# Moving the input tiles and four weight loads to other DMA queues in a linear-attention and MLP mixer

## The chip, the core and the metric

The kernel runs on one core of a Trainium2 chip. The core has five engines with a program each: TensorE (PE, matmuls; its weight loads are listed as PEld), VectorE (DVE), ScalarE (ACT), GpSimd (POOL) and SyncE (SP). Transfers between the main memory and the on-chip memory, and transposes by DMA, are issued by an engine into that engine's queue: SyncE and ScalarE have a hardware queue each (q1 and q10 in the profile), GpSimd a software one (q0). All queues are served by the same 16 DMA engines. An engine's issues go out in program order, and each may wait for semaphores first.

The metric is the device time of one execution in microseconds (us). Three runs of the kernel before took 259.40, 259.89 and 271.33 us; the median is 259.89.

## The reference

There are 2048 tokens of 640 features. A gate mixes two branches of the same input x:

```python
g = sigmoid((x * gate_w).sum(-1, keepdims=True))
a = A_ref(x, A_wqkv, A_wo)
b = B_ref(x, B_w1, B_w2, B_w3, B_w4)
return g * a + (1 - g) * b

# A: linear attention, 32 heads of 20
q, k, v = heads(x @ wqkv)
pq, pk = phi(q), phi(k)          # phi(t) = where(t > 0, t + 1, exp(t)) + 1e-6
kv = einsum("bhsd,bhse->bhde", pk, v);  z = pk.sum over tokens
o = (pq @ kv) / (pq . z + 1e-6)
a = o @ wo
# B: shifted MLP
h = gelu(layernorm(x) @ w1)      # its four quarters are shifted by +1, -1, +2, -2 tokens
x1 = x + shifted(h) @ w2
b = x1 + gelu(layernorm(x1) @ w3) @ w4
```

The inputs are bf16. w1 and w2 are 640 x 640, w3 is 640 x 1728, w4 is 1728 x 640, wqkv is 640 x 1920.

## The kernel before

Tokens are worked on in 16 tiles of 128. Features lie on the 128 partitions in 5 blocks, so a product over 640 features is 5 matmuls.

**Order.** The program records each operation with what it reads and writes; semaphore waits follow from overlaps of these. The order on each engine is that of recording. The loads and turns of x and a few constants are recorded first, line by line (lines 692 to 762). Everything after that is an item with a planned duration and due times (`IT.add`), and `_Items.run` chooses the next item by a cost model. An item that holds only DMAs takes its place on its queue by this choice. A wait at the head of an engine's program holds up all that was recorded behind it on that engine.

**Phase A** (to about 53 us): x tiles are loaded token by token into `x_tok` (`load_x`, line 680). Tiles 0 to 2 are transposed on PE. Tiles 3 to 15 are transposed by DMA from `x_tok` into `xT` on SyncE (`x_turn`, line 689): one "turn" per tile. There are four turn semaphores, so turn t waits for turn t - 4. Per tile, `q_tile` and `k_tile` multiply the turned tile (as PE's loaded weights) with wq and wk; ScalarE takes the exponential and VectorE finishes phi. Once per four tiles `q_turned` makes the last 128 q features, which a DMA turn (`q_back`, from `mT` to `pq_tok`) brings back to token order.

**Phase B** (to about 77 us): PE accumulates G = x^T pk (`gt_step`, `gt_tail`; part of it comes back by a DMA turn into `GT`, line 825), and `kvt_group` (line 993) multiplies G with wv into the heads' kv. Meanwhile GpSimd normalises x tiles into three slots `xn` (`normalize`), and SyncE turns them into `xnT` (`t_xn`, line 871).

**Phase C**: `w1_group` and `w2_tile` make x1; the second layer norm is turned in the same manner; `w3_group`, `w4_tile` and the attention's product with `M_sb` make the output. `m_last` and `m_first` read wo.

**Loads.** The weights of q and k are loaded at the start over the queues of SyncE and ScalarE. w1, w2, wv and wo are loaded over GpSimd's queue in three items (`lw1`, `lw2`, `lwv`): 8, 8 and 6 issues, each item behind the phi of key tile 7, 9 or 11 (`k_done`). w3 and w4 are loaded over SyncE's queue in two items (`w3load`, `w4load`) that stand behind the last turns of the first layer norm; w4 lies in memory that phase A and B use for other things, w3 in memory of its own.

Of the kernel before, what the change touches and what calls it, by code (L numbers as in the profile page):

```python
# [11 lines left out]
D = 640  # L12
F = 1728
H = 32
DH = 20
NT = S // 128
NCH = S // 512
# [5 lines left out]
B3 = 60  # L23
# [393 lines left out]
def _build(nc, A_x, A_wqkv, A_wo, B_w1, B_w2, B_w3, B_w4, gate_w, out, dbg=None, stop=None):  # L417
    sch = _Sched(nc)
# [55 lines left out]
    w3 = pa.alloc("w3", [128, KD, F], BF16)  # L474
    w1 = pa.alloc("w1", [128, KD, D], BF16)
    w2 = pa.alloc("w2", [128, KD, D], BF16)
    wo_aug = pa.alloc("wo_aug", [128, 6, D], BF16)
    x_tok = pa.alloc("x_tok", [128, NT, D], BF16)
# [23 lines left out]
    wv = wvf[:, 0:KD * D].rearrange("p (k d) -> p k d", d=D)  # L502
# [159 lines left out]
    def memset(engf, ap, val):  # L662
        return engf(lambda e: e.memset(ap, val), [], [ap])
# [11 lines left out]
    x2 = A_x[0]  # L675

    def dma_in(out_ap, in_ap, key, **kw):
        return sch.dma("sp", out_ap, in_ap, key, **kw)

    def load_x(t):  # L680
        dma_in(x_tok[:, t, :], x2[128 * t:128 * (t + 1), :], "x%d" % t)

    def load_wq(k, queue):
        sch.dma(queue, wq[:, k, 0:512], A_wqkv[128 * k:128 * (k + 1), 0:512], "wq%d" % k)

# [3 lines left out]
    def x_turn(t):  # L689
        sch.dma("sp", xT[:, :, 128 * t:128 * (t + 1)], x_tok[:, t, :], "trx%d" % (t % 4), transpose=True)  # L690

    gwr = xn[:, 1, 0:128]
    dve(lambda e: e.memset(gwr, 0.0), [], [gwr])
    load_x(0)
    load_wq(0, "act")
    load_x(1)
    load_wq(1, "act")
    load_wq(2, "sp")
    load_wq(3, "act")
    load_x(2)  # L700
# [6 lines left out]
    load_wk(2, "sp")  # L707
    load_wk(4, "sp")
    load_x(4)
    x_turn(3)  # L710
    load_x(5)
    sch.dma("pool", xn[0:KD, 1, 0:128], gate_w.rearrange("(k p) -> k p", p=128), "gw")
    x_turn(4)
    x_turn(5)
    for t0, t1 in ((6, 10), (10, NT)):
        dma_in(x_tok[:, t0:t1, :], x2[128 * t0:128 * t1, :].rearrange("(n p) d -> p n d", p=128), "xc%d" % t0)
        for t in range(t0, t1):
            x_turn(t)

    k_done = {}  # L720

    def load_w1():
        dp = [k_done[7]]
        for g_ in range(4):
            sch.dma("pool", w1[:, :, 128 * g_:128 * (g_ + 1)],
                    B_w1[:, 160 * g_:160 * g_ + 128].rearrange("(k p) f -> p k f", p=128), "w1", group_total=8, deps=dp)
            sch.dma("pool", w1[:, :, 512 + 32 * g_:512 + 32 * (g_ + 1)],
                    B_w1[:, 160 * g_ + 128:160 * (g_ + 1)].rearrange("(k p) f -> p k f", p=128), "w1", group_total=8, deps=dp)

    def load_w2():  # L730
        dp = [k_done[9]]
        for g_ in range(4):
            sch.dma("pool", w2[:, g_, :], B_w2[160 * g_:160 * g_ + 128, :], "w2", group_total=8, deps=dp)
            sch.dma("pool", w2[32 * g_:32 * (g_ + 1), 4, :], B_w2[160 * g_ + 128:160 * (g_ + 1), :], "w2", group_total=8, deps=dp)

    def wo_rows(h, e, ns):
        v = A_wo[0:600, :].rearrange("(q p) d -> p q d", p=B3)
        q0 = 2 * h + e
        return v[:, q0:q0 + 4 * (ns - 1) + 1:4, :]

    def load_wvo():
        dp = [k_done[11]]
        sch.dma("pool", wv[:, :, :], A_wqkv[:, 2 * D:3 * D].rearrange("(k p) f -> p k f", p=128), "wv", deps=dp)
        for h in range(2):
            for e in range(2):
                ns = 3 - h
                sch.dma("pool", wo_aug[64 * h:64 * h + B3, e:e + 2 * ns - 1:2, :],
                        wo_rows(h, e, ns), "wo", group_total=5, deps=dp)
        sch.dma("pool", wo_aug[64:104, 4, :], A_wo[600:D, :], "wo", group_total=5, deps=dp)

    memset(pool, ones_c[:], 1.0)
    memset(pool, wkg[:, :, D:D + 1], 1.0)
# [7 lines left out]
    memset(pool, wvf[:, KD * D:], 0.0)  # L760
    memset(pool, hsT[:, :, 0:4], 0.0)
    memset(pool, hsT[:, :, S:S + 4], 0.0)


    tags = {}
# [7 lines left out]
    IT = _Items()  # L773
# [41 lines left out]
    def gt_tail(t):  # L815
        if t == 0:
            gt_bank["t"] = pair()
            bank_hold.update((gt_bank["t"], gt_bank["t"] + 1))
        b = gt_bank["t"]
        for o, n0, n1 in ((ps[:, b, 0:512], 0, 512), (ps[:, b + 1, 0:128], 512, D)):  # L820
            gt_acc(o, [(pk_tok[:, t, 512:D], x_tok[:, t, n0:n1])], t)
        if t == NT - 1:
            bank_hold.difference_update((b, b + 1))
            activation(Mt[:, :], psf[:, 512 * b:512 * b + D], ACTF.Copy)
            sch.dma("sp", GT[:, :, 512:D], Mt[:, :], "trg", transpose=True)
# [45 lines left out]
    def t_xn(which, t):  # L871
        sx = xn_slots[(which, t)]
        tag_chk("xn", sx, (which, t))
        sch.dma("sp", xnT[:, :, 128 * t:128 * (t + 1)], xn[:, sx, :], "trn%d" % slot("trn", 4), transpose=True)
# [66 lines left out]
    def addA(name, dur, fn, deps=()):  # L941
        IT.add("A", name, dur, fn, deps)
# [7 lines left out]
    for i in range(3, NT + 2):  # L950
        if i < NT:
            addA(("q", i), 1.08, lambda t=i: q_tile(t))
            addA(("k", i), 1.36, lambda t=i: k_tile(t))
            if i % 4 == 3:
                addA(("qx", i // 4), 1.08, lambda c=i // 4: q_turned(c))
                IT.add("QB", ("qb", i // 4), 0.0, lambda c=i // 4: q_back(c),
                       deps=[(("qx", i // 4), 2.5), (("t1", NT - 1), 0.0) if i == NT - 1 else (("k", i + 1), 0.0)])
        if i > 3:
            for t in range(3) if i == 4 else (i - 2,):
                addA(("g0", t), 0.27, lambda t=t: gt_tail(t), deps=[(("k", max(t, 1)), 2.0)])  # L960

    IT.add("LW", ("lw1",), 0.0, load_w1, deps=[(("k", 7), 0.0)])
    IT.add("LW", ("lw2",), 0.0, load_w2, deps=[(("k", 9), 0.0)])
    IT.add("LW", ("lwv",), 0.0, load_wvo, deps=[(("k", 11), 0.0)])

    def stats1(c):
        ln_chunk_stats(st1, c, lr[:, 4 * c:4 * c + 4, 0:1].rearrange("p t o -> p (t o)"))
# [140 lines left out]
    def w3_group(c, j):  # L1108
        cols = slice(512 * c, 512 * (c + 1))
        sl = c % 2  # L1110
        if j == 0:
            tag_set("h2T", sl, c)
        b = bank()
        mm_group(ps[:, b, :], [(w3[:, k, 128 * j:128 * (j + 1)], xnT[:, k, cols]) for k in range(KD)])
        activation(h2T[:, j, 512 * sl:512 * (sl + 1)], ps[:, b, :], ACTF.Gelu_apprx_tanh)
# [177 lines left out]
        for n0, n1 in ((0, 384), (384, D)) if t0 == NT - 1 else ((0, D),):  # L1293
            sch.dma("act" if n1 == 384 else "sp", dst[:, :, n0:n1], x_tok[:, t0:t1, n0:n1], "out%d" % slot("out", 4))

    def w3_load():
        dma_in(w3[:, :, 0:F], B_w3.rearrange("(k p) f -> p k f", p=128), "w3")

    def w4_load():
        dma_in(w4[:, 0:KFF, :], B_w4[0:128 * KFF, :].rearrange("(k p) f -> p k f", p=128), "w4a")  # L1300
        dma_in(w4[0:64, KFF, :], B_w4[128 * KFF:F, :], "w4b")
        dma_in(w4[64:128, KFF, :], B_w4[128 * KFF:F, :], "w4c")
# [3 lines left out]
    for c in range(NCH):  # L1306
        for j in range(KD):
            deps = [(("t1", u), 0.9) for u in range(4 * c, 4 * c + 4)] if j == 0 else []
# [7 lines left out]
    for t in range(NT):  # L1316
        c = t // 4
        deps = [(("w1", c, KD - 1), GEL)]
# [8 lines left out]
    for u in range(NT):  # L1327
        deps = [(("s2", u // 4), 3.2 + 0.9 * (u % 4))]
# [3 lines left out]
            deps.append((("t1", NT - 3 + u), 0.0))  # L1332
        IT.add("N2", ("n2", u), 0.0, lambda u=u: normalize(2, u, st2), deps)
        IT.add("T2", ("t2", u), 0.0, lambda u=u: t_xn(2, u), deps=[(("n2", u), 1.1)] + ([(("mt",), 0.0)] if u == 12 else []))
    IT.add("MISC", ("w3load",), 0.0, w3_load, deps=[(("qb", NCH - 1), 0.0), (("k", NT - 1), 0.0), (("t1", NT - 1), 0.0)])
    IT.add("MISC", ("w4load",), 0.0, w4_load, deps=[(("qb", NCH - 1), 0.0), (("kvt", 1), 0.0), (("t1", NT - 1), 0.0), (("z", NT - 1), 1.5)])
    for c in range(NCH):
        for j in range(KFF):
            deps = []
            if c == 0 and j == 0:  # L1340
                deps0 = [(("kvt", 1), 0.0), (("z", NT - 1), 1.5)]
            else:
                deps0 = []
            if j == 0:
                deps = deps0 + [(("t2", u), 0.9) for u in range(4 * c, 4 * c + 4)]
                deps.append((("w3load",), 0.0))
                if c >= 2:
                    deps.append((("w4", (5, 11)[c - 2]), 0.0))
            if c == 0 and j == 3:
                deps.append((("w2", NT - 1), 0.0))  # L1350
            if c == 1 and 7 <= j <= 10:
                deps.append((("a", j - 7), 0.0))
            IT.add("W3", ("w3", c, j), 1.08, lambda c=c, j=j: w3_group(c, j), deps)
            if c == 1 and j == KFF - 1:
                for c2 in (0, 2):
                    IT.add("W3", ("w3h", c2), 1.14, lambda c2=c2: w3_half(c2), [(("t2", u), 0.9) for u in range(4 * c2 + 4, 4 * c2 + 8)] + [(("a", 3), 0.0)])
                IT.add("W3", ("w4h", 0), 0.76, lambda: w4_half(0), [(("w4load",), 0.0), (("a", 3), 0.0)])
    for t in range(NT):
        deps = [(("zb",), 1.0), (("q", max(t, 2)), 2.0), (("sg", 1), 0.0)]
# [13 lines left out]
    for t in range(NT):  # L1373
        g = GOF[t]
        t0, t1 = GROUPS[g]
        cl = (t1 - 1) // 4
        deps = [(("qt", t), 3.0), (("w4load",), 0.0), (("m", 1), 1.0), (("mt",), 2.5)]
# [65 lines left out]
```

## Time and profile before

The profiled execution took 259.2 us; its span, from the first instruction to the last, is 257.9 us.

| | |
|---|---|
| granted clock of TensorE | 1.00 in the whole span |
| DMA moved | 26.50 MB, mean 103 GB/s |
| SyncE's queue (q1) | 21.87 MB, 40.2% of the 16 engines' span |
| GpSimd's queue (q0) | 3.28 MB, 5.8% |
| ScalarE's queue (q10) | 1.11 MB, 1.4% |
| w3, 2160 KB, issued at 87.89 us | 8.1 us from issue to landing |
| w4's main part, 2080 KB, issued right behind it | 15.2 us |
| x tiles 6 to 9, 640 KB | 4.6 us |
| x tiles 10 to 15, 960 KB | 5.3 us |
| turns of x (xT) | 2.6 to 7.2 us, median 2.7 |

An engine's busy time counts its instructions but not its sequencer's work: waits, branches, DMA issues. All of SyncE is sequencer, so it has no busy time; its rows tell when a DMA was issued and how long the issue took. The time from issue to landing is that of one DMA, with the time that it stood behind others in its queue. The chain is followed back from the last instruction to whatever released each step.

### The profile page before, as it was taken

To read this page: it belongs to the slowest core of one execution; us is meant where nothing else is said; L and a number is where in the kernel's file an instruction comes from. 1 tells how busy PE (TensorE), PEld (TensorE's weight loads), DVE (VectorE), ACT (ScalarE), POOL (GpSimd) and SP (SyncE) were. 2 spreads that over 40 slices of the span, in tenths; PEclk is the share of its full clock that TensorE was granted. 3 is DMA by queue.
4 is the path that set the end of the run, shared out by engine and by line. 5 is a ranking of instruction groups with operands and counts; after the bars stand their busy time and mean duration, and the time that the engine had idled before them with its cause. 6 is when DMAs were issued, how large, how long until landed. Compare 5 with 4: busy or idle time off the path is not lost.

```text
span 257.9 us, 3904 instructions
## 1 busy us (share of the span) xinstructions
PE 255.1 (99%) x1478; PEld 126.7 (49%) x1478; DVE 144.8 (56%) x289; ACT 108.9 (42%) x224; POOL 90.9 (35%) x144
## 2 busy tenths in 40 slices
PE   8999999999999999999999999999999999999996
PEld 4555555544454545555444445444444744444744
DVE  2697888899964995589999300399700033200033
ACT  1587676651366868666854331001540100253100
POOL 5020499976952162677908000123200021300000
PEclk9999999999999999999999999999999999999999
DMA  7856699956637699372628630114130022200012
GB/s 226 226 135 114 188 137 177 262 109 126 127 76 79 125 399 293 84 100 56 121 49 117 123 60 3 31 25 127 36 17 0 3 52 80 102 1 3 0 20 102
DMA packets 57650, 26.50 MB, mean 103 GB/s; under 512 B 48884, under 2 KB 56221, under 8 KB 57632
## 3 DMA queue, kind: packets, MB, share of 16 engines
q1 hardware_dynamic: 54800, 21.87, 40.2%
q0 software_dynamic: 1168, 3.28, 5.8%
q10 hardware_dynamic: 1664, 1.11, 1.4%
q8 instruction: 11, 0.18, 0.3%
q14 instruction: 7, 0.06, 0.1%
HBM read 12.04 MB, written 2.62 MB: 57 GB/s over the span
## 4 chain that ended last, share of the span: by engine, by line
PE 99%; DVE 0%; issue 0%
PE ps L604 53%; PE ps L1213 30%; PE ps L811 8%; PE ps L922 2%; PE ps L884 1%; PE ps L1240 1%; PE ps L1128 1%; PE ps L615 1%; PE ps L1009 0%; PE ps L1038 0%; PE ps L923 0%; DVE x_tok L643 0%
## 5 line engine op out<-in xcount | busy, mean ns | idle before, releaser
L604 PE MATMUL ps<-xnT,w 128*128 128x512 bf16 x360 | 81.3, 379 | 0.0
L643 DVE SCALAR_TENSOR_TENSOR x_tok<-ps,stg,abx 128x512 bf16<-128x512 f32 (+2 forms) x17 | 12.2, 718 | 81.4 <-PE ps L1213 81.3
L660 ACT ACTIVATE h2T<-ps 128x512 bf16<-128x512 f32 x52 | 30.6, 598 | 59.5 <-PE ps L604 59.5
L604 PEld LDWEIGHTS ps<-xnT,w 128*128 128x128 bf16 x360 | 34.5, 98 | 39.8 <-issue 0.5
L1213 PE MATMUL ps<-w,h2T 128*128 128x512 bf16 (+2 forms) x221 | 45.4, 366 | 0.0
L626 POOL TENSOR_SCALAR xn<-x_tok,st 128x640 bf16<-128x640 bf16 x32 | 36.0, 1130 | 25.4 <-DMA xnT<-xn 24.9
L626 POOL TENSOR_SCALAR abx<-x_tok,stg 128x640 f32<-128x640 bf16 x16 | 15.3, 965 | 70.7 <-DVE x_tok L643 70.7
L1213 PEld LDWEIGHTS ps<-w,h2T 128*128 128x128 bf16 x221 | 21.2, 98 | 23.5
L660 ACT ACTIVATE Er<-ps 128x512 bf16<-128x512 f32 (+1 forms) x36 | 23.0, 649 | 14.6 <-PE ps L604 10.3
L659 ACT ACTIVATE junk<-x_tok 128x640 bf16<-128x640 bf16 x32 | 23.6, 738 | 3.9 <-DVE x_tok L641 3.7
L660 ACT ACTIVATE hsT<-ps 128x512 bf16<-128x512 f32 (+1 forms) x32 | 19.0, 594 | 12.5 <-PE ps L604 12.0
L604 PE MATMUL ps<-w,hsT 128*128 128x512 bf16 (+1 forms) x160 | 23.7, 299 | 0.0
L604 PE MATMUL ps<-wkg,xT 128*128 128x130 bf16 (+1 forms) x140 | 21.4, 299 | 0.0
L641 DVE SCALAR_TENSOR_TENSOR x_tok<-ps,x_tok 128x640 bf16<-128x640 f32 x16 | 13.1, 821 | 11.2 <-PE ps L604 10.5
L604 PEld LDWEIGHTS ps<-w,hsT 128*128 128x128 bf16 x160 | 13.3, 98 | 12.3
L1213 PE MATMUL ps<-M_sb,pqnT 128*128 128x512 bf16 (+2 forms) x85 | 18.6, 367 | 0.0
L811 PE MATMUL ps<-pk_tok,x_tok 128*128 128x512 bf16 x80 | 17.8, 379 | 0.0
L604 PEld LDWEIGHTS ps<-wkg,xT 128*128 128x128 bf16 x140 | 11.9, 97 | 11.4
L1157 DVE TENSOR_TENSOR pq_tok<-pq_tok,dnr 128x300 bf16<-128x300 bf16 (+1 forms) x48 | 16.9, 405 | 0.5
L634 DVE TENSOR_TENSOR qprod<-qprod,pk_tok 128x640 f32<-128x640 f32 x13 | 16.3, 1252 | 0.4
L626 DVE TENSOR_SCALAR Er<-Er 128x512 bf16<-128x512 bf16 (+1 forms) x36 | 12.3, 341 | 6.9 <-ACT Er L660 6.2
L604 PE MATMUL ps<-wq,xT 128*128 128x512 bf16 x65 | 16.2, 379 | 0.0
(87 smaller groups left out, 243.8 us busy)
## 6 DMA issues: line engine op xcount, KB each, us to landing
w<-in_B_w_dram SPq DMA_DIRECT2D x1, 2160.0 KB, 8.1
w<-in_B_w_dram SPq DMA_DIRECT2D x1, 2080.0 KB, 15.2
out_dram<-x_tok SPq DMA_DIRECT2D x3, 640.0 KB, 3.2
w<-in_B_w_dram POOLq DMA_DIRECT2D x8, 160.0 KB, 6.4
x_tok<-in_A_x_dram SPq DMA_DIRECT2D x6, 160.0 KB, 3.7
x_tok<-in_A_x_dram SPq DMA_DIRECT2D x1, 960.0 KB, 5.3
wv<-in_A_wqkv_dram POOLq DMA_DIRECT2D x1, 800.0 KB, 5.7
x_tok<-in_A_x_dram SPq DMA_DIRECT2D x1, 640.0 KB, 4.6
```

What stands on the lines that cost most here:

```text
L604: ins = e.matmul(out_ap, l, r, start=(i == 0), stop=(i == n - 1))
L615: ins = e.transpose(o, s_, ident[:])
L626: return engf(lambda e: e.tensor_scalar(out_ap, in_ap, s1, s2, op0, op1), rd, [out_ap], cost=cost)
L634: return engf(lambda e: e.tensor_tensor(out_ap, a, b_, op), [a, b_], [out_ap], cost=cost)
L641: return dve(lambda e: e.scalar_tensor_tensor(out_ap, in0, scalar, in1, op0, op1, accum_out=accum), rd, [out_ap, accum], cost=cost + 70.0)
L643: return dve(lambda e: e.scalar_tensor_tensor(out_ap, in0, scalar, in1, op0, op1), rd, [out_ap], cost=cost)
L659: return act(lambda e: e.activation(out_ap, in_ap, func, bias=bias, scale=scale, accum_out=accum), rd, wr, cost=cost)
L660: return act(lambda e: e.activation(out_ap, in_ap, func, bias=bias, scale=scale), rd, wr, cost=cost)
L811: ins = e.matmul(o, l, r, start=(t0 + q_ == 0), stop=(t0 + q_ == NT - 1))
L922: ins = e.matmul(ps[:, b, 0:512], l, w[:, k, 0:512], start=(k == 0), stop=(k == KD - 1))
L1157: dve(lambda e, o=o, i0=i0, i1=i1: e.tensor_tensor(o, i0, i1, ALU.mult), [i0, dnr[:, 1, sd, :]], [o], cost=cost)
L1213: ins = e.matmul(o, l, r, start=first and i == 0, stop=last and i == len(prs) - 1, skip_group_check=True)
```

## The change

Three things move; no operation on data is added or removed.

- x tile 5 (160 KB) and x tiles 6 to 9 (640 KB) are loaded over ScalarE's queue, behind the loads that stand there already. They wait for nothing.
- x tiles 10 to 15 (960 KB) are still loaded over SyncE's queue, now between turns 7 and 8 instead of behind turn 9.
- w1, w2, wv, wo and w3 are loaded over SyncE's queue, recorded behind the constants, so they stand behind turn 15 on that queue and wait for no other engine. The three items of GpSimd's loads and the item of w3 are gone; the first `w3_group` no longer names w3's item as a condition, the wait for the data remains. w4 is loaded as before.

Per engine, the instructions of PE, VectorE and ScalarE keep their order, apart from the two new issues on ScalarE ahead of its first table load. GpSimd loses its 22 issues, and eight of its normalisations come ahead of the last statistics of the first layer norm, where it was one. On SyncE the 23 issues stand between turn 15 and the first turn of `mT`; behind the three turns of `mT` come eight turns into `xnT`, then the turn into `GT`, then four more (before: the turn into `GT`, then ten).

```diff
+    def load_xs(queue, t0, t1):
+        sch.dma(queue, x_tok[:, t0:t1, :], x2[128 * t0:128 * t1, :].rearrange("(n p) d -> p n d", p=128), "xc%d" % t0)
...
     load_x(4)
-    x_turn(3)
-    load_x(5)
+    load_xs("act", 5, 6)
+    load_xs("act", 6, 10)
     sch.dma("pool", xn[0:KD, 1, 0:128], gate_w.rearrange("(k p) -> k p", p=128), "gw")
-    x_turn(4)
-    x_turn(5)
-    for t0, t1 in ((6, 10), (10, NT)):
-        dma_in(x_tok[:, t0:t1, :], x2[128 * t0:128 * t1, :].rearrange("(n p) d -> p n d", p=128), "xc%d" % t0)
-        for t in range(t0, t1):
-            x_turn(t)
+    for t in range(3, 8):
+        x_turn(t)
+    load_xs("sp", 10, NT)
+    for t in range(8, NT):
+        x_turn(t)
...
     def load_w1():
-        dp = [k_done[7]]
         for g_ in range(4):
-            sch.dma("pool", w1[:, :, 128 * g_:128 * (g_ + 1)],
-                    B_w1[:, 160 * g_:160 * g_ + 128].rearrange("(k p) f -> p k f", p=128), "w1", group_total=8, deps=dp)
-            sch.dma("pool", w1[:, :, 512 + 32 * g_:512 + 32 * (g_ + 1)],
-                    B_w1[:, 160 * g_ + 128:160 * (g_ + 1)].rearrange("(k p) f -> p k f", p=128), "w1", group_total=8, deps=dp)
+            dma_in(w1[:, :, 128 * g_:128 * (g_ + 1)],
+                   B_w1[:, 160 * g_:160 * g_ + 128].rearrange("(k p) f -> p k f", p=128), "w1", group_total=8)
+            dma_in(w1[:, :, 512 + 32 * g_:512 + 32 * (g_ + 1)],
+                   B_w1[:, 160 * g_ + 128:160 * (g_ + 1)].rearrange("(k p) f -> p k f", p=128), "w1", group_total=8)
...
     memset(pool, hsT[:, :, S:S + 4], 0.0)
+    load_w1()
+    load_w2()
+    load_wvo()
+    dma_in(w3[:, :, 0:F], B_w3.rearrange("(k p) f -> p k f", p=128), "w3")
...
-    IT.add("LW", ("lw1",), 0.0, load_w1, deps=[(("k", 7), 0.0)])
-    IT.add("LW", ("lw2",), 0.0, load_w2, deps=[(("k", 9), 0.0)])
-    IT.add("LW", ("lwv",), 0.0, load_wvo, deps=[(("k", 11), 0.0)])
...
-    def w3_load():
-        dma_in(w3[:, :, 0:F], B_w3.rearrange("(k p) f -> p k f", p=128), "w3")
...
-    IT.add("MISC", ("w3load",), 0.0, w3_load, deps=[(("qb", NCH - 1), 0.0), (("k", NT - 1), 0.0), (("t1", NT - 1), 0.0)])
...
-                deps.append((("w3load",), 0.0))
```

`load_w2` and `load_wvo` change as `load_w1` does.

## The prediction

> **What bounds the kernel now.** I read the page first: the span, the busy shares and the chain that ended last.
>
> ```profile
> span 257.9 us, 3904 instructions
> PE 255.1 (99%) x1478; PEld 126.7 (49%) x1478; DVE 144.8 (56%) x289; ACT 108.9 (42%) x224; POOL 90.9 (35%) x144
> PE 99%; DVE 0%; issue 0%
> ```
>
> TensorE is on the chain from end to end. A busy PE need not be a fast one, so the pace comes next, from the chain in order of time (start, length, what; this stretch holds the places that the change can reach late).
>
> ```profile
> 69.82 4.32 PE ps L604 x20
> 74.13 1.08 PE ps L811 x5
> 75.21 1.08 PE ps L604 x5
> 76.29 1.06 PE ps L1009 x50
> ```
>
> Twenty 512-column matmuls in 4.32 us are 0.216 us each; no stretch of the chain after 12 us is slower per matmul, and the waits of PE list one wait, 0.8 us at the start. The changed program issues the same PE, DVE and ACT compute in the same order, so the time falls only if the first 12 us shrink. There, L922 takes 1.67 us for 7 and 1.88 us for 8 matmuls, 0.3 us above 15 x 0.216; that 0.3 us is the largest gain to be had, and the change brings nothing earlier that those matmuls read. What remains is a loss: wherever a transfer is late for PE, PE has no later idle time to make it up, and the loss stands in the end time.
>
> So I read for each moved transfer when PE needs it. SyncE's own rows (issues; "us" runs to the end of the last of the row):
>
> ```profile
> 8.75 1.30 SPq L281 DMA_TRANSPOSE xT<-x_tok  x1
> 10.10 0.57 SPq L285 DMA_DIRECT2D x_tok<-in_A_x_dram  x1
> 10.83 3.01 SPq L281 DMA_TRANSPOSE xT<-x_tok  x2
> 13.89 0.58 SPq L285 DMA_DIRECT2D x_tok<-in_A_x_dram  x1
> 18.50 5.18 SPq L281 DMA_TRANSPOSE xT<-x_tok  x4
> 23.72 0.58 SPq L285 DMA_DIRECT2D x_tok<-in_A_x_dram  x1
> 29.07 8.30 SPq L281 DMA_TRANSPOSE xT<-x_tok  x6
> 37.41 6.68 SPq L281 DMA_TRANSPOSE pq_tok<-mT  x3
> 56.77 1.20 SPq L281 DMA_TRANSPOSE GT<-Mt  x1
> ```
>
> Turn 3 issues at 8.75 and lands 2.65 us later, at 11.41. PE's weight loads of q tile 3 start at 13.01, those of q tile 4 at 16.37. Slack of turn 3: 1.6 us. That is the smallest among the x turns.
>
> **x5 to x9 on ScalarE's queue.** Two issues of 0.46 us (ACT's median row) follow ACT's last load, 3.65 to 4.11, so they end near 5.05. Behind them on ACT waits the table load (4.14, 1.28 us), now over at 6.33; the first Exp waits for PE until 7.73. That cover is 1.4 us, so the issues cost nothing. The data (160 + 640 KB = 0.82 MB) queue behind ACT's own loads, which end by about 10, and share the DMA engines with what SyncE's queue still holds. These answers give the rates (busy us of the engines, granted clock, DMA share, GB/s; then the queues between 8 and 10.05 us):
>
> ```profile
> 4.00:8.00 4.00, 4.00 (x27) 2.10 (x26) 1.84 (x8) 1.55 (x2) 0.72 (x5) 1.00 1.03 339
> 8.00:10.00 2.00, 2.00 (x13) 0.94 (x12) 1.74 (x6) 1.41 (x3) 0.00 (x0) 1.00 0.77 230
> ```
>
> ```profile
> q1 hardware_dynamic: 329, 0.36, 54.8%
> q10 hardware_dynamic: 369, 0.10, 21.0%
> ```
>
> With both queues full the engines moved 339 GB/s, so 0.82 MB is 2.4 us of all 16. Left at 8.0 us: SyncE's queue (q1) 0.548 x 2.05 = 1.1 us, ScalarE's (q10) 0.21 x 2.05 = 0.4 us, x5 to x9 2.4 us, turn 3 0.8 us (between 18 and 24 us 2261 packets took 46.7% of 6 us, 0.83 us per turn of 672). Sum 4.7: all done at 12.7, and on the last engine about a us later, since the share falls off slowly between 9 and 10 us. If the queues alternate, turn 3 ends with the last of it and lands 0.5 us after (as it does now), 13.2 to 14.2; if SyncE's queue went first, it would stay at 11.4. Against 13.01 that is a stall of 0 to 1.2 us. The key weights wk2 and wk4 are nearer to the front of SyncE's queue (landing 9.42 and 10.24, read at 9.46 and 10.83): at most 0.4 us late, and that would come off the turn's stall. I take **0.6 us**: equal sharing is what the first us show (between 3.4 and 4.9 us the two queues have 50.8% and 47.1%). The outer bound is the worst turn of this trace under another queue's load, 7.2 us to landing: 8.75 + 7.2 = 15.95, a stall of 2.9 us. The stall at q tile 3 moves all later needs along with it.
>
> Turn 4 waits for x4 (10.82, perhaps 11.3 now) and lands by 15, before 16.37. Turn 5 no longer has a load in front of it. Turns 6 and 7 wait for one transfer that lands near 14.8 instead of 18.48. The 960 KB load goes out behind turn 7 at about 17.6 (5.33 us: 22.9); turns 8 and 9 queue behind its bytes and land near 24.2, for q tiles at 29.2 and later; turns 10 to 15 issue from 22.9 to 30.8 and land by 32 against 43.3 now. All earlier, nothing on the path: PE takes the tiles at its own pace.
>
> The Trainium skill's DMA: Bandwidth & Descriptors (Issuing engines are not separate DMA queues) says that a second queue saves the sequencer's time to issue and nothing else. By that rule the gain is two issues of 0.57 us on SyncE, and x6 to x9 would land 1.15 us earlier; by the rows they land 3.7 us earlier, since SyncE's issue stood in order behind waits. Either is worth 0 to the end time.
>
> **The weights on SyncE's queue.** Removed from POOL: 22 issues, 31.9 to 43.3 and 46.3 to 50.5, about 15 us of an engine off the path: 0. Added to SyncE: 22 issues and w3, 0.43 to 0.58 us each, 9.9 to 13.3 us, from 30.8: w3 issues at about 43 and lands 8.1 us later, 51. The bytes agree: w1 as 2560 runs of 256 B and as many of 64 B, of which the 256 B cost 0.21 x 2.05 x 16 / 369 = 18.7 ns now (q10 above, mostly such packets) and the 64 B at most that: 4.5 to 6 us; w2, wv, wo 0.82 MB each at 334 to 339 GB/s, 7.3 us; w3 2.2 MB, 6.5 us; 18.3 to 19.8 from 32, the same 51. If each small packet costs what the turns' packets cost under load (86.0% of 7.1 us for 2279, 43 ns), w1 is 13.7 us and the end is 59.
>
> Behind w3 on the queue stand three turns of mT, the first normalised tiles (8), GT and the rest. By my times: mT 55, tile 0 at 56.3, tile 3 at 60.1 (POOL refills three slots, 1.3 us a tile), tile 7 at 65.4, GT at 66.7. Now tile 3 lands at 64.6, GT at 59.3. PE needs tile 3 at 69.8 and GT at 76.3: slack 9.7 and 9.6 us: 0. At the 59 bound 2 us are left: still 0. POOL no longer waits behind 22 issues, and w1, w2, wv lie 18 us or more ahead of their readers. w3's place before w4 (87.89 to 96) is gone, so w4 and the tiles behind it (7.99 us to landing now) come 6 us or more earlier: no PE wait there to remove, 0.
>
> **Sum.** The profiled execution took 259.2 us, 1.3 more than its span; the three runs had 259.4, 259.89 and 271.33, so it lies 0.7 under the median. 259.2 + 0.6 = **259.8 us**; the case's own bounds are 258.9 (the 0.3 of the start) and 260.4.
>
> **The rivals.**
> - *Turns 3 and 4 suffer more from sharing* than by equal parts: up to the 2.9 us above, 260.4 to 262.1. For: turns 14 and 15 took 7.1 and 7.2 us to landing beside POOL's loads. Against: those stood behind other turns too. 0.12.
> - *Slower: the weights hold up the turns behind them.* One place, SyncE's queue from 32 us on: every us that w3 lands past 51 + 9.6 = 60.6 makes PE wait a us at 69.8 or 76.3. It decides over 2% (5.2 us) past 65.8. For: six loads, 5.4 MB, in front of everything, and a 5.43 us blocked issue at 89.08 behind w3 and w4. Against: the bounds above, 51 to 59. 264 to 270 us. 0.12. The first matmuls (L884) run 3456 columns in 3.04 us, 0.88 ns a column against 0.42 later. On that, TensorE: Matmul & The Clock Gate (Part 1) has the array fall back to half its clock after an idle window of some 3.4 us; no run here shows such a gap, and by the page this case would cost up to 1.7 us more.
> - *ScalarE's queue is full* and the second issue blocks, as SyncE's did at 89.08, until its loads are through at about 10: table load to 11.3, first Exp 3.6 us late, and PE short of PSUM banks: 1 to 3.5 us, 260.2 to 262.7. Against: the instruction that overfilled SyncE's queue (88.51) itself took 0.53; the next one blocked, and ACT has no next DMA. 0.04.
> - *Faster by over 2%*: PE would have to do its 255 us in less. 0.02.
>
> **Chances.** Main case 0.70. Within 2% (about what a measurement of this kernel can tell from no change): main, the first rival and most of the third, 0.85. Slower 0.13, faster 0.02. The range, 258.8 to 263.0, holds the main case, the first and third rivals, about 0.85, and leaves out the slower one and the faster.
>
> **What would show it.** Right: a PE wait of 0.3 to 1.2 us before the weight loads of q tile 3, on the turn; turn 3 landing at 13 to 14; turns 10 to 15 landed by 33; w3 landing at 49 to 53; GT at 64 to 69; PE without a wait after 14 us. Wrong: a PE wait at 69.8, 76.3 or anywhere later; the first Exp after 8; matmuls at another pace than 0.216 us.

## The result, and the profile after

The kernel after took 262.18 us (median of 6 runs, 261.54 to 262.65), beside 259.78 for the kernel before (median of 6, 259.08 to 271.33). The ratio is 1.0100, with a 95% interval of 1.0077 to 1.0123. (The medians and ranges count all runs; the ratios leave out those more than 1.5% above the fastest of their kernel, which only the kernels with before's loads over GpSimd's queue had.) So the change costs 1%: less than the 2% that were taken as the bound of a change, but clear of zero. On another chip the same two kernels gave 262.44 and 259.86, ratio 1.0084 [1.0057, 1.0112]. The profiled execution after took 261.74 us, 2.5 more than the one before.

The page of after, with the span, the busy shares and the chain that ended last:

```profile
span 260.5 us, 3904 instructions
PE 255.5 (98%) x1478; PEld 126.3 (48%) x1478; DVE 139.0 (53%) x289; ACT 109.1 (42%) x224; POOL 74.5 (29%) x122
PE 77%; DMA 10%; POOL 6%; DVE 5%; SPq 1%; ACT 1%; issue 1%; DVEq 0%
```

TensorE works as long as before (255.5 against 255.1 us), but it no longer fills the chain: 21% of the span now belongs to transfers, GpSimd and VectorE. The waits of PE after (what waited, for what; us in total, times, longest):

```profile
PE ps L886 <- PEq L1421: 0.8, 1, 0.8
PE ps L1036 <- DVE x_tok L641: 0.7, 1, 0.7
PE ps L604 <- DVE x_tok L641: 0.6, 1, 0.6
PE ps L924 <- DMA wq<-in_A_wqkv_dram: 0.5, 1, 0.5
PE ps L604 <- DMA xT<-x_tok: 0.2, 1, 0.2
```

The first line is the wait that stood in before. The last two are arrivals at the start: wq2 landed at 6.55 instead of 5.70 us, and q tile 3 waited for turn 3. The two on VectorE (`x_tok`, line 641, is the evacuation of the second MLP product from PSUM, the banks that TensorE writes its products to) are new, and they lie near 95 us, where nothing had been expected. The chain of after in order of time (start, length, what) leads there:

```profile
9.40 4.65 DMA xT<-x_tok
14.10 6.13 PE ps L604 x35
...
53.98 5.57 DMA xnT<-xn
59.55 0.09 issue
59.64 6.86 POOL xn L626 x5
66.50 0.73 POOL st L626
...
72.03 2.13 POOL xn L626 x3
74.17 2.71 DMA xnT<-xn
...
78.14 3.45 DMA zb<-zsum
...
81.61 0.83 DVE zc L1070
...
83.23 2.55 DMA zb<-zsum
...
85.88 0.84 DVE qprod L634
...
96.83 30.22 PE ps L604 x180
```

GpSimd normalises tiles 3 to 7 first and only then, at 66.50, takes up the last statistics of the layer norm; tiles 8 to 11 are recorded behind these and start at 72.03. SyncE's turns of those tiles stand in front of one that has nothing to do with them: the first turn of `zsum` (the token sum z, into `zb`). SyncE's rows of after and of before show it (issues):

```profile
44.84 9.10 SPq L281 DMA_TRANSPOSE pq_tok<-mT  x3
53.98 13.74 SPq L281 DMA_TRANSPOSE xnT<-xn  x8
67.77 1.28 SPq L281 DMA_TRANSPOSE GT<-Mt  x1
72.92 5.18 SPq L281 DMA_TRANSPOSE xnT<-xn  x4
78.14 1.27 SPq L281 DMA_TRANSPOSE zb<-zsum  x1
```

```profile
58.02 13.46 SPq L281 DMA_TRANSPOSE xnT<-xn  x10
73.78 1.20 SPq L281 DMA_TRANSPOSE zb<-zsum  x1
```

Before, `zsum` was turned behind tile 9 and landed at 76.35; after, behind tile 11, landing at 81.59. Its data were ready at 71.5 us, earlier than before (73.8, when the turn went out at once). VectorE's rows, before and after, show who waits (the bracket is the idle time ahead of the row and what ended it):

```profile
76.38 0.82 DVE L1072 TENSOR_REDUCE zc<-zb 128x5 f32<-128x640 bf16 x1 [1.85 <-DMA zb<-zsum]
...
82.10 0.82 DVE L641 SCALAR_TENSOR_TENSOR x_tok<-ps,x_tok 128x640 bf16<-128x640 f32 x1 [3.75 <-PE ps L604]
...
82.84 0.82 DVE L634 TENSOR_TENSOR qprod<-pq_tok,zb 128x640 f32<-128x640 bf16 x1
...
99.38 0.82 DVE L641 SCALAR_TENSOR_TENSOR x_tok<-ps,x_tok 128x640 bf16<-128x640 f32 x1 [2.68 <-PE ps L604]
```

```profile
70.65 0.83 DVE L634 TENSOR_TENSOR zsum<-qprod,pk_tok 128x640 bf16<-128x640 f32 x1
...
81.61 0.82 DVE L1070 TENSOR_REDUCE zc<-zb 128x5 f32<-128x640 bf16 x1 [9.56 <-DMA zb<-zsum]
...
83.32 0.83 DVE L641 SCALAR_TENSOR_TENSOR x_tok<-ps,x_tok 128x640 bf16<-128x640 f32 x1
...
85.88 0.83 DVE L634 TENSOR_TENSOR qprod<-pq_tok,zb 128x640 f32<-128x640 bf16 x1 [1.72 <-DMA zb<-zsum]
```

Before, VectorE twice stood waiting for PE at an evacuation (3.75 and 2.68 us): it was ahead. After, it stands 9.56 us at the head of `zc`, and 1.72 us more at the head of `qprod`: z goes over SyncE's queue twice. VectorE reduces the first turn's result (`zc`), ScalarE writes that back into `zsum`, and a second turn brings it into `zb`, where `qprod` reads it. ScalarE's row of that copy, before and after:

```profile
79.28 0.73 ACT L660 ACTIVATE zsum<-zc 128x640 bf16<-128x640 f32 x1
```

```profile
82.47 0.74 ACT L660 ACTIVATE zsum<-zc 128x640 bf16<-128x640 f32 x1 [2.04 <-DVE zc L1070]
```

Before, the copy started 2.1 us after `zc` was done, behind evacuations of ScalarE's own; after, it starts as soon as `zc` is done. From 85.88 on VectorE works without a gap, and the evacuations that are recorded among this work do not catch up before PE needs the PSUM banks again.

**Where the 2.5 us went.** Both kernels run PE's instructions in the same order, so the start of one matmul can be compared. PE's lag is read at two places: the first product with `hsT` (80.54 us before) and the first with `M_sb` (138.07 before), one on each side of the two new waits. After has them at 81.58 and 140.62: 1.04 us late already from q tile 3 on, 2.55 late past the waits. So 1.04 us came from the start, 1.51 from `zsum`, and 259.2 + 1.04 + 1.51 = 261.75, against 261.74 measured.

### The profile page after: what moved, and what is told of

It reads as the page before. It is cut to its first block, busy times and chain, and to the rows that moved or that the text cites. A ratio compares the mean times of both kernels' runs of the same rounds, so it can differ in the third digit from the quotient of the medians.

```text
span 260.5 us, 3904 instructions
## 1 busy us (share of the span) xinstructions
PE 255.5 (98%) x1478; PEld 126.3 (48%) x1478; DVE 139.0 (53%) x289; ACT 109.1 (42%) x224; POOL 74.5 (29%) x122
## 4 chain that ended last, share of the span: by engine, by line
PE 77%; DMA 10%; POOL 6%; DVE 5%; SPq 1%; ACT 1%; issue 1%; DVEq 0%
PE ps L604 43%; PE ps L1211 30%; POOL xn L626 4%; DMA xnT<-xn 3%; DMA x_tok<-in_A_x_dram 2%; DMA zb<-zsum 2%; DMA xT<-x_tok 2%; PE ps L813 1%; POOL st L634 1%; DVE x_tok L641 1%; PE ps L1238 1%; DVE dnr L1136 1%; DVE qprod L634 1%; PE ps L1126 1%; SPq L285 1%; DVE pq_tok L1155 1%
## 5 line engine op out<-in xcount | busy, mean ns | idle before, releaser
L626 POOL TENSOR_SCALAR xn<-x_tok,st 128x640 bf16<-128x640 bf16 x32 | 33.6, 1058 | 31.4 <-DMA xnT<-xn 31.0
L660 ACT ACTIVATE Er<-ps 128x512 bf16<-128x512 f32 (+1 forms) x36 | 23.2, 646 | 14.1 <-PE ps L604 10.5
L626 DVE TENSOR_SCALAR Er<-Er 128x512 bf16<-128x512 bf16 (+1 forms) x36 | 11.3, 313 | 8.0 <-ACT Er L660 7.1
L660 ACT ACTIVATE mw<-ps 128x384 bf16<-128x384 f32 (+1 forms) x6 | 2.7, 456 | 28.5 <-PE ps L1211 28.5
```

The costliest lines, as they stand in the source:

```text
L626: return engf(lambda e: e.tensor_scalar(out_ap, in_ap, s1, s2, op0, op1), rd, [out_ap], cost=cost)
L660: return act(lambda e: e.activation(out_ap, in_ap, func, bias=bias, scale=scale), rd, wr, cost=cost)
```

## The experiments

All profiles below are read by these two lags. "Before" in a ratio is the kernel before on the same chip as the run.

**Each half alone.** One kernel makes only the edits of the x tiles (the planner then records the same order as before):

```diff
-    x_turn(3)
-    load_x(5)
+    load_xs("act", 5, 6)
+    load_xs("act", 6, 10)
...
+    for t in range(3, 8):
+        x_turn(t)
+    load_xs("sp", 10, NT)
+    for t in range(8, NT):
+        x_turn(t)
```

> Only the x loads move (x5 to x9 to ScalarE's queue, x10 to x15 behind turn 7); the weights load as before. Theory 'two causes' (1.04 us lost before 14.1 us by sharing the DMA engines, 1.5 us lost at 82 to 97 us by a late turn of zsum): 1.0 us over before, PE about 0.6 us late at its first key matmul and about 1.0 late at q tile 3, no wait of PE after 15 us. Rival 'start differs from run to run': the first key matmul at 8.96 us as before, only the wait for turn 3, 0.4 us over before. Rival 'all of it is the x part': 2.5 us over before.

Measured: 260.40 us (259.78 to 260.94, 12 runs), ratio 0.9995 [0.9963, 1.0027]. Lag 1.36 us at the first place and 1.37 at the second: all of it made by q tile 3, nothing later. A loss of 1.0 us had been expected; the profile has it, the times do not show it, and with before's own spread the interval leaves room for -1.0 to +0.7 us.

The other makes only the edits of the weights:

```diff
-    IT.add("LW", ("lw1",), 0.0, load_w1, deps=[(("k", 7), 0.0)])
-    IT.add("LW", ("lw2",), 0.0, load_w2, deps=[(("k", 9), 0.0)])
-    IT.add("LW", ("lwv",), 0.0, load_wvo, deps=[(("k", 11), 0.0)])
...
+    load_w1()
+    load_w2()
+    load_wvo()
+    dma_in(w3[:, :, 0:F], B_w3.rearrange("(k p) f -> p k f", p=128), "w3")
```

> Only the weights move to SyncE's queue; x loads as before. Theory 'two causes': no wait before 15 us; the first turn of zsum issued near 77 us and landing near 80 instead of 76.35, and PE late by 1 to 2 us at the first wo matmuls (L1036) and behind them. The rival 'all of it is the x part' says equal to before within 0.3 us.

Measured: 266.38 us (265.04 to 266.47, 6 runs), ratio 1.0215 [1.0168, 1.0261]; the interval reaches to both sides of 2%. That is far more than the 1 to 2 us that were expected. Without the x edits the last turn of x lands at 41.42 us instead of 32.57, the weights start 9 us later, and w3 lands at 65.39 (55.99 in after). Tile 3 into `xnT` then lands at 72.15 and PE stands still. TensorE in stretches (us, busy with count of matmuls, granted clock, DMA share, GB/s):

```profile
66.00:70.00 4.00, 4.00 (x20) 1.00 0.67 133
70.00:72.00 2.00, 0.31 (x2) 1.00 0.72 146
72.00:74.00 2.00, 1.60 (x7) 0.88 0.52 104
74.00:76.00 2.00, 2.00 (x7) 0.50 0.74 147
76.00:78.00 2.00, 2.00 (x9) 0.77 0.50 99
```

The lag grows here from 0.49 to 4.42 us: 2.25 us of standing still (a matmul starts 2.47 us after the one before it instead of 0.22), and 1.7 us because nine matmuls then start up to 0.43 us apart, half the pace, under a granted clock of 0.50. Another 2.69 us go where `zsum` is late (it lands at 86.16). So the halves don't add: the weights alone cost 2%, the x edits alone nothing that the times show, and both together 1%, because the x edits make room on SyncE's queue for the weights (w3 lands 9.4 us earlier with them).

**The order pinned, in two ways.** Both kernels are the kernel after, weights on SyncE's queue, with one condition more for the planner. The first puts GpSimd's statistics of tiles 12 to 15 ahead of its tile 1, as they were in before; `zsum`'s turn then falls behind tile 9 again:

```diff
+        if u == 1:
+            d1.append((("s1", 3), 0.0))
```

> The changed kernel with one more condition in the planner: the second normalised tile comes behind the last statistics of the first layer norm. GpSimd's order is then that of before, and on SyncE the first turn of zsum stands behind turn 9 into xnT as before (only the turn into GT stands behind turn 0 instead of ahead of it). All weights are still ahead of these turns on SyncE's queue. Theory 'order' (the late turn of zsum comes from its recorded place behind turns 8 to 11 and from the statistics behind tile 7): first turn of zsum lands at 77 to 78, the 1.5 us at 82 to 97 go, 1.0 to 1.1 us over before. Rival 'queue' (w3's bytes ahead of the turns make them late, whatever the order): zsum's turn still lands after 80, 2 to 2.5 us over before.

The second leaves GpSimd's order as in after and changes SyncE's alone: the turn of tile 8 goes behind that of `zsum`.

```diff
-        IT.add("T1", ("t1", u), 0.0, lambda u=u: t_xn(1, u), deps=[(("n1", u), 1.1)] + ([(("zb",), 0.0)] if u == 12 else []))
+        IT.add("T1", ("t1", u), 0.0, lambda u=u: t_xn(1, u), deps=[(("n1", u), 1.1)] + ([(("zb",), 0.0)] if u == 12 else []) + ([(("zt",), 0.0)] if u == 8 else []))
```

> The changed kernel with SyncE's order alone altered: the first turn of zsum ahead of turn 8 into xnT instead of behind turn 11; GpSimd's order stays as in the changed kernel. Theory 'order on SyncE': zsum is ready near 72 us, its turn lands near 75, PE waits nowhere at 82 to 97: 1.0 to 1.1 us over before. Rival 'late statistics on GpSimd' (the tiles 8 to 11 themselves come too late): PE still waits 1 us or more between 82 and 97 us, 2 us or more over before.

Measured: 260.37 us (259.48 to 261.11, 12 runs), ratio 0.9997 [0.9969, 1.0025], for the first; 260.45 (259.74 to 260.95, 12 runs), ratio 1.0000 [0.9970, 1.0029], for the second. SyncE's rows of the first, then of the second:

```profile
58.02 2.37 SPq L281 DMA_TRANSPOSE GT<-Mt  x1
60.44 12.27 SPq L281 DMA_TRANSPOSE xnT<-xn  x9
75.01 1.20 SPq L281 DMA_TRANSPOSE zb<-zsum  x1
```

```profile
66.75 1.28 SPq L281 DMA_TRANSPOSE GT<-Mt  x1
71.33 1.20 SPq L281 DMA_TRANSPOSE zb<-zsum  x1
72.58 5.25 SPq L281 DMA_TRANSPOSE xnT<-xn  x4
```

In the second `GT` goes out at 66.75 and tile 8 at 72.58, about as late as in after (67.77 and 72.92); `zsum` goes out 6.8 us earlier, and PE's lag is 1.01 us at the first place and 1.02 at the second (first `hsT` matmul 81.55, first `M_sb` matmul 139.09). In the first it is 1.25 and 1.26. The two waits on VectorE are gone in both. The waits of PE in the first that are left, besides the one at the start:

```profile
PE ps L604 <- DMA xT<-x_tok: 0.5, 1, 0.5
PE ps L615 <- DMA x_tok<-in_A_x_dram: 0.3, 1, 0.3
PE ps L924 <- DMA wq<-in_A_wqkv_dram: 0.3, 1, 0.3
```

So, with the bytes of the weights where the change put them, the place of one turn in SyncE's order makes the 1.51 us or takes them away.

**The same order in the kernel before.** If that is so, the old kernel must get slower by the late turn alone. Here everything is as in before, but behind the planner's work `zsum`'s turn and the two turns after it in SyncE's program change places:

```diff
+    sp_ = sch.prog["sp"]
+    i_ = next(k for k, e_ in enumerate(sp_) if e_[2] == "d:trz")
+    z_, p_, q_ = sp_[i_:i_ + 3]
...
+    sp_[i_:i_ + 3] = [(z_[0] + p_[0], p_[1], p_[2]), q_, z_]
```

> The kernel before, with one thing altered: on SyncE the first turn of zsum stands behind turns 10 and 11 into xnT instead of ahead of them; turn 10 waits for zsum as it does in the kernel before. Weights, x loads and the order on all other engines as before. Theory 'order': the turn lands 3 to 4 us later, near 80; VectorE, which waits for it in its program order, falls behind, and PE waits 1 to 2.5 us between 82 and 97 us; 1 to 2.5 us over before. Rival 'queue' (only the weights ahead of the turns can cost time there): no wait of PE, equal to before.

Measured: 261.49 us (259.32 to 269.35, 12 runs) against 260.12, ratio 1.0042 [1.0011, 1.0073]. The lag is 0.40 at the first and 1.90 at the second place: 1.50 us lost between them. `zsum` landed at 80.85, and PE has the same two new waits:

```profile
PE ps L604 <- DVE x_tok L641: 0.8, 1, 0.8
PE ps L1038 <- DVE x_tok L641: 0.6, 1, 0.6
```

**The x tiles elsewhere.** Two versions of the pinned kernel keep x tiles 5 to 9 away from ScalarE's queue. In the first they are loaded over SyncE's queue behind turns 3 and 4:

```diff
-    load_xs("act", 5, 6)
-    load_xs("act", 6, 10)
+    x_turn(3)
+    load_x(5)
...
-    for t in range(3, 8):
+    x_turn(4)
+    load_xs("sp", 6, 10)
+    for t in range(5, 8):
```

> The kernel with the pinned statistics (label pin_s1), with x5 and x6 to x9 on SyncE's queue behind turns 3 and 4 instead of on ScalarE's queue. Theory 'sharing': turn 3 lands 2.6 to 2.7 us after its issue, PE does not wait at q tile 3, 0.4 to 0.8 us under pin_s1, no wait later. Rival 'sharing costs nothing, the late turn 3 has another cause': PE still waits there, equal to pin_s1.

In the second, over GpSimd's queue, once turn 3 has landed:

```diff
-    load_xs("act", 5, 6)
-    load_xs("act", 6, 10)
+    turn3 = x_turn(3)
...
+    load_xs("pool", 5, 6, [turn3])
+    load_xs("pool", 6, 10, [turn3])
```

> As sp_pin, but with x5 and x6 to x9 on GpSimd's queue, held until turn 3 has landed. Theory 'sharing': no wait at q tile 3, within 0.3 us of sp_pin. If the x tiles come too late by this queue, PE waits at q tile 5 or 6 instead.

Measured: 259.83 us (259.29 to 260.41, 12 runs), ratio 1.0003 [0.9981, 1.0024], and 259.88 (258.92 to 260.86, 12 runs), ratio 1.0010 [0.9986, 1.0034]. The lags are 0.07 and 0.08 us for the first. For the second they are 0.59 and 1.38, in an execution of 260.58 us, the third slowest of the twelve: its SyncE issues one turn every 1.32 us without a gap from 63 us on, and `zsum`, although pinned behind tile 9, lands only at 80.41. An order is no guarantee; the queue must also have the time.

**The kernel before, once more,** for how much the early arrivals differ between executions of one kernel.

> The kernel before once more, for its profile alone: when the first key matmul starts (8.96 us in the first profile; 9.59 in the changed kernel, 9.5 with the x loads alone). If the early 0.6 us belongs to the change, it starts at 8.8 to 9.1 again; if it differs from execution to execution, anywhere from 8.9 to 9.6.

It caught one of the executions that make before's range wide: 266.54 us (a single run). The first key matmul was 0.8 us later than in the first profile (9.76 us), so a late start there does not belong to the change alone. The larger part is later: the last six turns of x, which took up to 7.2 us to landing in the first profile, took up to 14.1 here, beside the loads of GpSimd's queue (SyncE's row of their issues, and the three times of all turns of x):

```profile
32.28 10.81 SPq L281 DMA_TRANSPOSE xT<-x_tok  x6
```

```profile
DMA to landing us min/median/max: 2.6/2.7/14.1
```

PE's lag was 5.38 us at the first place, 7.34 at the second.

**One chip for all.** The pinned versions and the kernel after had been timed on different chips, so the kernel after, the first pinned version and the version with x on SyncE's queue were run side by side.

> The changed kernel once more, beside two corrected versions and the kernel before on one chip, since the versions with a pinned order were timed on another chip than the changed kernel. Theory (the late turn of zsum costs 1.5 us, the shared arrival of x5 to x9 about 1 us): median 262.0 to 262.6, ratio 1.005 to 1.011, first turn of zsum landing at 80 to 82, two waits of PE on VectorE's evacuation of the w2 product, 0.5 to 0.9 us each, near 94 to 97. Rival (the difference was the chip's): the changed kernel is within 0.5 us of the pinned versions here, at about 260.

> The changed kernel with GpSimd's statistics of chunk 3 pinned ahead of tile 1 into xn again, on the same chip as the changed kernel. Theory: 1.5 us below the changed kernel (260.2 to 260.9), zsum's first turn landing at 77 to 78. Rival (chip): equal to the changed kernel.

> The pinned order and x5 to x9 back on SyncE's queue behind turns 3 and 4, on the same chip as the changed kernel. Theory: below the pinned version by the 0.6 us that q tile 3 waited there for its turn, so 259.4 to 260.2, and about 2.2 us below the changed kernel. Rival (the stall of q tile 3 is made up for later in the program): equal to the pinned version within 0.2 us.

Measured, against 259.86 for before (24 runs): 262.44 (260.93 to 263.01, 6 runs), ratio 1.0084 [1.0057, 1.0112]; 260.44 (259.57 to 261.19, 12 runs), ratio 1.0019 [0.9997, 1.0041]; 259.87 (258.82 to 260.93, 12 runs), ratio 0.9992 [0.9970, 1.0015]. The chip was not the cause. The order of GpSimd's statistics is worth 262.44 - 260.44 = 2.0 us here (`zsum` landed at 82.50, a us later than in the first profile of after), the place of x tiles 5 to 9 another 0.57. From the 12 runs of each, the means of these two lie 0.55 us apart, with a 95% interval of 0.1 to 1.0.

**All profiles together.** "From PE" is the landing of `zsum` less PE's lag at that time, so it is counted on PE's own clock.

| kernel | `zsum` lands | lag, first `hsT` | from PE | lag, first `M_sb` | lost between |
|---|---|---|---|---|---|
| before | 76.35 | 0 | 76.35 | 0 | 0 |
| after + tile 8 behind `zsum` | 73.90 | 1.01 | 72.89 | 1.02 | 0.01 |
| x edits alone | 77.69 | 1.36 | 76.33 | 1.37 | 0.01 |
| pinned statistics | 77.58 / 77.29 | 1.25 / 0.38 | 76.33 / 76.91 | 1.26 / 0.39 | 0.01 / 0.01 |
| pinned, x on SyncE | 76.78 / 77.31 | 0.07 / 0.69 | 76.71 / 76.62 | 0.08 / 0.70 | 0.01 / 0.01 |
| pinned, x on GpSimd | 80.41 | 0.59 | 79.82 | 1.38 | 0.79 |
| before + late turn | 80.85 | 0.40 | 80.45 | 1.90 | 1.50 |
| after | 81.59 / 82.50 | 1.04 / 1.13 | 80.55 / 81.37 | 2.55 / 3.46 | 1.51 / 2.33 |
| weights alone | 86.16 | 4.42 | 81.74 | 7.11 | 2.69 |
| before, second profile | 86.06 | 5.38 | 80.68 | 7.34 | 1.96 |

All rows up to 76.91 lose nothing; from 79.82 on, all but the last lose within 0.1 us what "from PE" lies past 79.05 (the last loses 0.3 more). In before the turn landed at 76.35, so it had 2.7 us of slack. The steps behind the turn show where it lay. On PE's clock, `qprod` starts at 82.84 in before and at 85.88 - 1.04 = 84.84 in after: of the 4.20 us by which the turn lands later, 2.00 are left. The other 2.2 were ScalarE's copy, which stood behind other work (2.04), and the second turn, which landed at 82.59, a little ahead of VectorE (0.15). Of the 2.00 PE loses 1.51, so 0.5 us lay between VectorE's evacuations and PE's need of the banks; in the second profile of after it is the same (2.82 and 2.33). VectorE's wait of 2.68 us at 99.38 is of the same size by chance: it lies behind the matmuls that come late.

## Why the prediction was wrong

**The bound and the pace** held: PE's work did not change, no stretch gained, and every us that PE lost stayed in the end time.

**The sum.** It starts from one profile of 259.2 us, which the prediction itself puts 0.7 under the median, and so arrives at the old median although it adds 0.6. From before's median, 259.78, the same term gives 260.4, which is where the pinned kernels with x on ScalarE's queue lie (260.37 to 260.45). The other 1.8 us to 262.18 are the term that it put at 0, below. That 262.18 lies inside the range of 258.8 to 263.0 is luck: the room in it was given for turns 3 and 4 and for ScalarE's queue.

**x5 to x9 on ScalarE's queue: right, in mechanism and size.** The queues of after between 10 and 14 us (packets, MB, share of 16 engines) show SyncE's queue sharing the engines with ScalarE's, which had 0.8% of them between 10 and 11.5 us before:

```profile
q1 hardware_dynamic: 1314, 0.40, 68.0%
q10 hardware_dynamic: 553, 0.66, 48.7%
```

Turn 3 took 4.65 us to landing instead of 2.65, as the sharing had it, and landed at 14.05 (13 to 14 were named). In the six profiles with these loads on ScalarE's queue it took 4.65 to 5.18 us, in the seven without 2.66 to 2.88. It also went out later, at 9.40 instead of 8.75, since x3 landed 0.65 us later; that part is not the change's, for x3 lands at 8.39 to 9.44 with these loads and at 8.74 to 9.55 without. The turn stalled q tile 3 by 0.43 us, in the other kernels with these loads on ScalarE's queue by 0.36 to 0.78. The six profiles with them there have a mean lag at the first `hsT` of (1.04 + 1.13 + 1.36 + 1.25 + 0.38 + 1.01) / 6 = 1.03 us. The seven without (the two kernels with long stalls taken ahead of these, at 0.49 and 0.80) have (0 + 0.40 + 0.07 + 0.69 + 0.59 + 0.49 + 0.80) / 7 = 0.43. The difference is 0.60 (the six spread over 1.0 us, the seven over 0.8), and the two medians on one chip say 0.57: the term that was taken. The 0.43 is what one profile hides: the profile of before that the sum was made from had the earliest start of the seven. The sign "the first Exp after 8" did come (8.35), but that Exp waited 1.60 us for PE, not for the two issues.

**Turns 10 to 15: right**, landed by 32.57. What this was worth was missed. It was put down as "all earlier, nothing on the path"; by the weights alone it is what keeps the weights off the path.

**The weights on SyncE's queue: the step that failed.** It found that w3 and what stands behind it cost 0, from two needs, tile 3 at 69.8 and `GT` at 76.3, and concluded "PE without a wait after 14 us". The two needs were met: w3 landed at 55.99 (51 was taken, the bound was 59), tile 3 at 63.41 and `GT` at 70.40. Both were later than predicted, but within the slack. The third client of the same queue, `zsum`'s turn, was never costed. Its new place could be read from the recorded order, which has `zsum` behind twelve turns into `xnT` where it stood behind ten; so could GpSimd's, where the last statistics went behind eight tiles. The order was told and no time was attached to it. The working ended at PE's own waits on transfers; here the first turn of `zsum` holds up VectorE and ScalarE, with them the second turn, and with that VectorE again; VectorE's program order then holds up the PSUM banks, and only these hold up PE, 13 us after the first turn landed. That chain costs 1.5 us in the first profile, 2.3 in the second. The two pins take it away with the weights where the change put them, and the late turn alone brings it into the kernel before.

**The slower rival** had named the right queue with the wrong item. In the form that it was given (w3 past 60.6), it is real only without the x edits: at 65.39 it is 4.8 us past that point, and PE lost 3.93 us there. The bound itself was too early where GpSimd's order is pinned: w3 landed at 61.05 and 63.12 in two such profiles (x on SyncE's queue, x on GpSimd's) and PE did not wait for it. Of the 3.93 us, 1.7 were half pace, with a granted clock of 0.50 from 73.51 to 76.92 us: the size of the prediction's estimate. The page that it was worked out from, the Trainium skill's TensorE: Matmul & The Clock Gate (Part 1), has the clock fall after an idle window of some 3.4 us. Here 2.25 us of standing still were enough: in the 3.4 us ahead of the fall PE was at work for the last 1.1 (from 72.40 on). Nor did the clock fall each time: over the whole span it was 0.994 in four of the six runs and 1.00 in two.

**What stays open.** Why x3 lands anywhere from 8.39 to 9.55 us, wherever the later x tiles are loaded, was not settled, nor which part of the early lag belongs to the loads of the k weights. That the planner chose the other order because the load items left it follows from the halves alone (the x edits keep the order, the weights change it); by which of its costs was not followed.

## What to carry to other kernels

When a change removes items from a planner, list every transfer whose place in a queue's order changed, and follow each to the engine that waits for it in program order and to what is recorded behind that wait; a slack counted only at TensorE misses the ones that act through VectorE and PSUM. Look for the slack link by link in the old trace, as the time by which each step's data lie ready before the step starts: here 2.0 us at ScalarE's copy, 0.2 at VectorE's product and 0.5 at the PSUM banks, 2.7 us in all. Two halves of a change may carry each other, so time each alone before one is dropped.

## What the runs showed that was not expected

- **The spread of before is a collision.** Before ranges from 259 us to between 267.8 and 271.3 in each set of runs; after and all others spread by 2.1 us or less, except the version with the late turn (10.0), which keeps before's loads. The halves separate it: x turns that have landed by 32.5 us, before GpSimd's loads go out at 33.3 (x edits alone), spread by 1.2 us, late turns without those loads (weights alone) by 1.4, late turns beside those loads (before) by 9 to 12. In the execution of before that took 266.54 us, the turns took up to 14.1 us to landing. So the change lowers the worst case (271.33 to 262.65) while it raises the median, and the pinned version with x on SyncE's queue has before's median with a range of 258.82 to 260.93 on one chip and 259.29 to 260.41 on another. No version's ratio lies clear of 1 on the faster side.
- **SyncE's issue can block behind a large load.** With w3 just issued, one of the three turns of `mT` took 6.41 us to issue in after and 7.56 us with the weights alone, against 1.2 to 1.3 us for a turn. The issue behind w4's main part, the blocked one that the prediction names at 89.08, took 5.43 us in before, with w3 ahead of w4, and 0.94 in after, without w3 there.
